# Two of four column transposes moved from TensorE to the DMA engines, with the head-row moves split over two queues

## Chip, cores, metric

One core of a Trainium2 chip. The metric is the device time of one execution in microseconds (us). TensorE is called PE, VectorE DVE, ScalarE ACT, GpSimd POOL or Pool, SyncE SP.

## The reference

```python
xn = layernorm(A_x)                                # 2048 rows of 512, bf16
# branch A: 32 heads of 16; each row attends to 8 rows before it, 2 apart
q, k, v = split(xn @ wqkv)
s = softmax(masked(q . k[i - 2w], w = 0..7) * 0.25) @ v[i - 2w]  @ wo
# branch B: layernorm, gelu(. @ w1), row shifts, @ w2, residual,
#           layernorm, gelu(. @ w3) @ w4, residual, silu
out = x + s * silu(B(xn))
```

## The kernel before

The rows are split by parity into two halves (p = 0, 1) of 1024, each in two chunks of 512. Chunks 0 and 1 are half 0, chunks 2 and 3 half 1. Queries and keys, and branch B's `w1`, need the normed rows as columns (`xnT`). PE makes all four chunks' columns by multiplying with the identity:

```python
def stage_t(c, h):                  # half a chunk: 8 PE transposes, one copy out
    ...
    for j in range(2):
        for dt in range(ND):
            nc.tensor.transpose(pt[:, dt, j, :], x_c[:, 2 * h + j, dt * P : (dt + 1) * P], ident[:])
    copy(out=xnT[p][:, :, t0 : t0 + 2 * P], in_=pt.rearrange("p a j q -> p a (j q)"))

def stage_m(c):                     # DVE: columns times the second norm's factor, for w1
    nc.vector.tensor_tensor(out=xn2T[c], in0=xnT[p][:, :, cs], in1=rrep..., op=ALU.mult)
```

The scores work on 32-row groups of which 16 rows are one head's and 16 the mask's. DVE fills whole tiles with the mask (`mask_fill`), and then small DMAs, the head-row moves, put the heads of `kq` into them, 64 to 72 KB each:

```python
def spread(p, lo, hi, q=nc.sync, ws=(0, 1)):       # w: keys, queries; 8 moves for each
    for w in ws:
        for e in range(2):
            for gr in range(4):
                r = 32 * gr + DH * e
                q.dma_start(out=(kT, qT)[w][e][r : r + DH, :, lo:hi], in_=kq[p][w][r : r + DH, :, lo:hi])
```

Issue order of the part in question (each engine runs its own instructions in this order):

```python
    stage_w1(0, 0); stage_t(1, 0); stage_t(1, 1)
    ln_stats(2); ln_again(2); stage_w1(0, 1)
    mask_fill(0); spread(0, 0, CH); ln_norm(2)            # 16 moves on SP
    ...                                                   # projections of chunk 1
    stage_t(2, 0); stage_t(2, 1)
    ln_stats(3, 0, 2); ln_stats(3, 2, 4); ln_norm(3); ln_again(3)
    stage_w1(1, 0); stage_w1(1, 1); stage_r(2); stage_m(2)
    qk_pair(2, 0); stage_t(3, 0); stage_t(3, 1); qk_pair(2, 1)
    stage_w1(2, 0, lambda: stage_r(3)); stage_m(3)
    mask_fill(1); spread(0, CH, X)                        # 16 moves on SP
    stage_w1(2, 1); load_w3(); stage_w1(3, 0); stage_w1(3, 1)
    va = values(0, 0)
    # then the first attention pass: 8 units of scores, values, w2 tiles, projections
```

The later feed-forward stage already makes columns by DMA: rows to a DRAM scratch (`x1n_dram`), and a transposing DMA back.

The softmax here doesn't subtract the row's maximum and nothing guards it: scores larger than these inputs give would overflow.

## Time and profile before

| | before |
|---|---|
| median time, all runs | 206.55 us |
| profiled span | 204.8 us, clock 0.998 |
| PE transposes of chunks 2 and 3 | 0.89 and 0.90 us |
| first score group of the first pass | 44.57 to 44.93 us |
| first pass from there to the feed-forward | 44.93 to 88.41 us |

The span runs from the first to the last instruction; the device time is 1.8 us longer. The prediction below shows the lines.

### The profile page before, as it was taken

Reading aid. Unit: us, or ns where it says so; the run is one execution under the profiler, and the core shown is the slowest. Engines: PE = TensorE matmul, PEld = TensorE weight load, DVE = VectorE, ACT = ScalarE, POOL = GpSimd, SP = SyncE. Lnnn points to the kernel's source line nnn. Section 1 sums busy time; section 2 is a strip of 40 time slices with the busy share of each in tenths; the row PEclk is TensorE's granted clock in tenths of the full one; section 3 lists DMA queues with packets and bytes.
Section 4 is the critical chain, followed back from the end, with each engine's and each line's share of the span. In section 5 each row is a group of like instructions: output and inputs, shape, how many; then the busy total and the mean of one; then the engine's idle time right before and its main releaser. Section 6 shows DMA issues by size and latency. Waiting matters only on the chain.

```text
span 204.8 us, 4854 instructions
## 1 busy us (share of the span) xinstructions
PE 197.3 (96%) x1944; PEld 95.6 (47%) x1944; DVE 135.2 (66%) x256; ACT 132.7 (65%) x160; POOL 74.1 (36%) x145
## 2 busy tenths in 40 slices
PE   7799999999999999999999999999999999999990
PEld 2475455444444444544444444444455544444440
DVE  5788996545487986776940001188577968888693
ACT  2366788868968687885556557898788877212130
POOL 4798465000032294933791000003830590700000
PEclk9999999999999999999999999999999999999999
DMA  5992065067900399485779948695130241554312
GB/s 131 361 349 84 15 101 96 0 97 113 293 10 0 108 121 151 86 212 105 180 178 215 286 145 134 93 254 193 34 54 3 52 92 26 122 162 135 95 51 77
DMA packets 30590, 25.69 MB, mean 125 GB/s; under 512 B 12505, under 2 KB 28481, under 8 KB 30569
## 3 DMA queue, kind: packets, MB, share of 16 engines
q1 hardware_dynamic: 28376, 22.17, 43.0%
q0 software_dynamic: 2048, 3.09, 8.9%
q8 instruction: 15, 0.25, 0.5%
q10 hardware_dynamic: 144, 0.13, 0.2%
q14 instruction: 7, 0.05, 0.1%
HBM read 12.40 MB, written 4.46 MB: 82 GB/s over the span
## 4 chain that ended last, share of the span: by engine, by line
PE 87%; ACT 4%; DVE 4%; POOL 1%; DMA 1%; issue 1%
PE w_ps L511 19%; PE w_ps L491 19%; PE qk_ps L391 8%; PE v_ps L537 7%; PE w_ps L424 7%; PE s_ps L557 6%; PE w_ps L447 6%; PE wo_ps L673 6%; PE o_ps L580 4%; PE qk_ps L409 4%; ACT arena L562 3%; PE tr_ps L353 1%; DMA arena<-in_A_x_dram 1%; ACT arena L414 1%; DVE l0s L304 1%; POOL l0r L308 1%
## 5 line engine op out<-in xcount | busy, mean ns | idle before, releaser
L562 ACT ACTIVATE arena<-s_ps 128x960 bf16<-128x960 f32 (+1 forms) x68 | 62.9, 979 | 14.4 <-PE s_ps L557 14.4
L511 PE MATMUL w_ps<-arena 128*128 128x512 bf16 (+1 forms) x164 | 39.1, 380 | 0.0
L496 ACT ACTIVATE arena<-w_ps 128x1024 bf16<-128x1024 f32 x20 | 20.5, 1023 | 15.0 <-PE w_ps L491 14.3
L491 PEld LDWEIGHTS <-arena 128*128 128x128 bf16 (+1 forms) x176 | 17.5, 100 | 20.6 <-issue 0.4
L622 POOL DMA_DIRECT2D arena<-orw x48 | 24.9, 527 | 5.8 <-DVE orw L592 5.8
L511 PEld LDWEIGHTS <-arena 128*128 128x128 bf16 (+1 forms) x176 | 16.5, 98 | 19.6
L683 POOL TENSOR_TENSOR arena<-arena 128x512 bf16<-128x512 bf16 x6 | 7.7, 1301 | 44.5 <-DVE arena L681 44.5
L526 ACT ACTIVATE sig<-arena 128x512 bf16<-128x512 bf16 x16 | 10.1, 630 | 20.8 <-DVE arena L517 20.7
L541 DVE CAST v_aug<-v_ps 128x512 bf16<-128x512 f32 x17 | 11.7, 688 | 14.6 <-PE v_ps L537 14.6
L592 DVE CAST orw<-o_ps 128x960 bf16<-128x960 f32 (+1 forms) x17 | 19.7, 1156 | 2.5 <-PE o_ps L580 2.4
L491 PE MATMUL w_ps<-arena 128*128 128x512 bf16 (+1 forms) x88 | 19.5, 379 | 0.1
L491 PE MATMUL w_ps<-arena,arena 128*128 128x512 bf16 (+1 forms) x88 | 19.2, 379 | 0.0
L391 PE MATMUL qk_ps<-arena 128*128 128x512 bf16 (+1 forms) x104 | 18.6, 330 | 0.5 <-ACT arena L321 0.5
L537 PE MATMUL v_ps<-wv_sb,arena 128*128 128x512 bf16 x68 | 17.5, 380 | 0.1
L557 PEld LDWEIGHTS <-arena 32*128 32x128 bf16 x544 | 10.1, 92 | 14.5 <-issue 14.4
L273 POOL TENSOR_SCALAR l3r<-l3m 128x1 f32<-128x1 f32 (+1 forms) x10 | 2.2, 222 | 39.0 <-DVE l3m L282 39.0
L557 PE MATMUL s_ps<-arena 32*128 32x120 bf16 (+1 forms) x544 | 15.8, 214 | 0.0
L447 PE MATMUL w_ps<-arena 128*128 128x512 bf16 x64 | 15.7, 380 | 0.1
L517 DVE TENSOR_TENSOR arena<-w_ps,arena 128x512 bf16<-128x512 f32 x16 | 11.0, 686 | 7.2 <-PE w_ps L511 7.2
L650 DVE TENSOR_TENSOR arena<-arena,orw 128x1440 bf16<-128x1440 bf16 (+1 forms) x2 | 1.6, 784 | 20.5 <-DMA orw<-rden_d 20.5
L424 PE MATMUL w_ps<-arena 128*128 128x512 bf16 x64 | 14.6, 379 | 0.0
L451 DVE TENSOR_TENSOR arena<-w_ps,arena 128x512 bf16<-128x512 f32 x16 | 10.7, 686 | 4.1 <-PE w_ps L447 4.1
(98 smaller groups left out, 278.9 us busy)
## 6 DMA issues: line engine op xcount, KB each, us to landing
x1n_dram<-arena SPq DMA_DIRECT2D x4, 512.0 KB, 3.0
arena<-in_A_x_dram SPq DMA_DIRECT2D x4, 512.0 KB, 6.1
arena<-in_A_x_dram SPq DMA_DIRECT2D x6, 256.0 KB, 7.0
out_dram<-arena SPq DMA_DIRECT2D x6, 256.0 KB, 3.0
arena<-in_B_w_dram SPq DMA_DIRECT2D x1, 1376.0 KB
arena<-in_B_w_dram SPq DMA_DIRECT2D x1, 1280.0 KB
arena<-arena SPq DMA_DIRECT2D x16, 72.0 KB, 2.6
arena<-arena SPq DMA_DIRECT2D x16, 68.0 KB, 3.5
```

Of the source, the lines that this page charges most:

```text
L391: nc.tensor.matmul(pt[:, b, hh * w : (hh + 1) * w], lhsT=wqk_sb[:, dt, nt * P : (nt + 1) * P], rhs=xnT[p][:, dt, k * CH + hh * w : k * CH ...
L424: nc.tensor.matmul(pt[:, b, :], lhsT=w1_sb[:, dt, g * P : (g + 1) * P], rhs=xn2T[c][:, dt, :], start=(dt == 0), stop=(dt == ND - 1),)
L447: nc.tensor.matmul(pt, lhsT=w2_src(p, g, m0), rhs=w2_sb[:, g, :], start=(g == 0), stop=(g == ND - 1))
L491: nc.tensor.matmul(pt[:fs, ft % 2, :], lhsT=w3_sb[:, dt, ft * P : ft * P + fs], rhs=x1nT[c][:, dt, :], start=(dt == 0), stop=(dt == ND - 1),)
L496: nc.scalar.activation(h3(c, 2 * a, 2), pt, AF.Gelu_apprx_tanh)
L511: nc.tensor.matmul(pt, lhsT=h3(c, ft, 1)[:fs, 0, jj * P : (jj + 1) * P], rhs=w4_sb[:fs, ft, :], start=(ft == 0), stop=(ft == NF - 1),)
L537: nc.tensor.matmul(vp[:nk, :], lhsT=xnT[p][:, dt, k0 : k0 + nk], rhs=wv_sb[:, dt, :], start=(dt == 0), stop=(dt == ND - 1),)
L557: nc.tensor.matmul(st[:nk, b, i * nq : (i + 1) * nq], lhsT=kT[e][r : r + 32, dt, k0 : k0 + nk], rhs=qT[e][r : r + 32, dt, q0 : q0 + nq], s ...
L562: nc.scalar.activation(prv[:nk, 2 * h : 2 * h + 2], st[:nk, :, 0 : 4 * nq], AF.Exp, scale=SCALE)
L592: nc.vector.tensor_copy(out=orw[p, r][:, :, :, q0 - ra : q0 - ra + nq], in_=op[:, :, 0 : 4 * nq].rearrange("p j (s q) -> p j s q", q=nq),)
L622: nc.gpsimd.dma_start(out=oT[p][DH * hh : DH * (hh + 1), :, ra : ra + rw], in_=orw[p, r][32 * cg : 32 * cg + DH, jj],)
L673: nc.tensor.matmul(pt, lhsT=oT[p][:, dt, i * P : (i + 1) * P], rhs=wo_sb[:, dt, :], start=(dt == 0), stop=(dt == ND - 1),)
```

## The change

Its intent: take 32 transposes off PE; norm chunks 2 and 3 earlier, so that their longer way through DRAM is hidden; give Pool most of the head-row moves, because SP now issues the transposes; move three projections out of the attention pass and regroup it; load the exp table ahead of the first exp.

```diff
+    def turn_dma(c, lo=0, hi=TPC):
+        rows = x1n_dram[c * CH + lo * P : c * CH + hi * P, :]
+        nc.sync.dma_start(out=rows..., in_=xn[p][:, k * TPC + lo : k * TPC + hi, :])
+        return lambda: nc.sync.dma_start_transpose(
+            out=xnT[p][:, :, k * CH + lo * P : k * CH + hi * P], in_=rows)
 ...
     stage_t(1, 0)
     stage_t(1, 1)
-    ln_stats(2)
+    ln_stats(2, 2, 4)
+    mask_full(0)
+    ln_norm(2)
+    turn_dma(2)()
     ln_again(2)
 ...
+    ln_norm(3, slice(0, 1))
+    turns = [turn_dma(3, 0, 2)]
+    ln_stats(3, 2, 4)
+    mask_fill(0, (0,))
+    ln_norm(3, slice(1, 2))
+    turns.append(turn_dma(3, 2, 4))
+    for f in turns:
+        f()
+    ln_again(3)
+    spread(0, 0, CH, nc.gpsimd, (0,))
 ...
-    stage_t(2, 0)
-    stage_t(2, 1)
 ...
+    mask_fill(0, (1,))
+    spread(0, 0, CH, nc.gpsimd, (1,), (0,))
     qk_pair(2, 0)[0]()
-    stage_t(3, 0)
-    stage_t(3, 1)
     qk_pair(2, 1)[0]()
+    spread(0, 0, CH, nc.sync, (1,), (1,))
+    mask_fill(1, (0,))
+    spread(0, CH, X, nc.gpsimd, (0,))
 ...
+    spread(0, CH, X, nc.sync, (1,))
     stage_w1(2, 1)
+    qk_pair(2, 2)[0]()
 ...
+    qk_one(2, 6)
+    nc.scalar.preload_act_table_set("exp_and_others")
-        (("www", "qq"), ("q", "ww"), ("qw", "qw"), ...)
+        [("www", "qw")] + [("q", "ww")] * 6 + [("q", "q")]
```

(Cut: moved statistics and mask pieces, `values(0, 0)` moved ahead of `stage_r(2)`, shifted places of a few small items in the pass and of one pair of later moves, the start of one buffer rotation.)

More of the change, by code (lines that the diff above doesn't have):

```diff
@@ L113 @@
     sg_at = (61, 66, B0 + 33.5)
-    cnt = {"v": 0, "p": 1, "b": 0, "r": 0, "g": 0}
+    cnt = {"v": 0, "p": 0, "b": 0, "r": 0, "g": 0}
     def pst(tag, name):
@@ L238, in mask_full, with mask_fill @@
         )
-    def mask_fill(k):
-        for w in range(2):
+    def mask_fill(k, ws=(0, 1)):
+        for w in ws:
             for e in range(2):
@@ L247, in mask_fill, with spread @@
                     )
-    def spread(p, lo, hi, q=nc.sync, ws=(0, 1)):
+    def spread(p, lo, hi, q=nc.sync, ws=(0, 1), es=(0, 1)):
         for w in ws:
-            for e in range(2):
+            for e in es:
                 for gr in range(4):
@@ L321, in first_t, with ln_norm @@
         nc.scalar.copy(out=xnT[0][:, :, j * P : (j + 1) * P], in_=pt)
-    def ln_norm(c):
+    def ln_norm(c, part=slice(None)):
         p, k = c // 2, c % 2
         x_c = xn[p][:, k * TPC : (k + 1) * TPC, :]
-        for lo, hi, mv, rstd in lns[c]:
+        for lo, hi, mv, rstd in lns[c][part]:
             for j in range(lo, hi):
@@ L356, in stage_t @@
         copy(out=xnT[p][:, :, t0 : t0 + 2 * P], in_=pt.rearrange("p a j q -> p a (j q)"))
+    def turn_dma(c, lo=0, hi=TPC):
+        p, k = c // 2, c % 2
+        rows = x1n_dram[c * CH + lo * P : c * CH + hi * P, :]
+        nc.sync.dma_start(
+            out=rows.rearrange("(i q) d -> q i d", q=P), in_=xn[p][:, k * TPC + lo : k * TPC + hi, :]
+        )
+        return lambda: nc.sync.dma_start_transpose(
+            out=xnT[p][:, :, k * CH + lo * P : k * CH + hi * P], in_=rows
+        )
     def stage_x():
@@ L726 @@
     ln_norm(1)
-    mask_full(0)
-    mask_full(1)
     parts[1][1]()
@@ L731 @@
     qk_pair(0, 3)[0]()
+    ln_stats(2, 0, 2)
     stage_w1(0, 0)
@@ L734 @@
     stage_t(1, 1)
-    ln_stats(2)
+    ln_stats(2, 2, 4)
+    mask_full(0)
+    ln_norm(2)
+    turn_dma(2)()
     ln_again(2)
     stage_w1(0, 1)
-    mask_fill(0)
-    spread(0, 0, CH)
-    ln_norm(2)
+    ln_stats(3, 0, 2)
+    mask_full(1)
     for a in range(2):
@@ L747 @@
     stage_x()
-    stage_t(2, 0)
-    stage_t(2, 1)
-    ln_stats(3, 0, 2)
-    ln_stats(3, 2, 4)
-    ln_norm(3)
-    ln_again(3)
     stage_w1(1, 0)
     stage_w1(1, 1)
+    va = values(0, 0)
     stage_r(2)
     stage_m(2)
+    mask_fill(0, (1,))
+    spread(0, 0, CH, nc.gpsimd, (1,), (0,))
     qk_pair(2, 0)[0]()
-    stage_t(3, 0)
-    stage_t(3, 1)
     qk_pair(2, 1)[0]()
+    spread(0, 0, CH, nc.sync, (1,), (1,))
+    mask_fill(1, (0,))
+    spread(0, CH, X, nc.gpsimd, (0,))
     stage_w1(2, 0, lambda: stage_r(3))
     stage_m(3)
-    mask_fill(1)
-    spread(0, CH, X)
+    mask_fill(1, (1,))
+    spread(0, CH, X, nc.sync, (1,))
     stage_w1(2, 1)
+    qk_pair(2, 2)[0]()
     load_w3()
@@ L769 @@
     stage_w1(3, 1)
-    va = values(0, 0)
+    qk_one(2, 6)
+    nc.scalar.preload_act_table_set("exp_and_others")
     groups = {n: ([], []) for n in range(len(order))}
@@ L778 @@
     w2q = [lambda t=t: w2_and(t) for t in range(S // P)]
-    qkq = [lambda t=t: qk_one(2 + t // 8, t % 8) for t in range(4, 16)]
+    qkq = [lambda t=t: qk_one(2 + t // 8, t % 8) for t in range(7, 16)]
     for n, (a, b) in enumerate(
-        (("www", "qq"), ("q", "ww"), ("qw", "qw"), ("q", "ww"), ("qw", "qw"), ("q", "ww"), ("qw", "qw"), ("q", "w"))
+        [("www", "qw")] + [("q", "ww")] * 6 + [("q", "q")]
     ):
@@ L796 @@
     st3(3, 4)
-    st3(4, 5, 6, 7)
+    st3(4, 5, 6)
+    st3(5, 7)
     late[6] += [lambda: ln3_norm(1), lambda: normalise_dn(0, 1), lambda: ln3_turn(1)]
@@ L834 @@
     for w in range(2):
-        late[3 + w].append(lambda w=w: spread(1, 0, CUT, nc.gpsimd, (w,)))
+        late[3 + 2 * w].append(lambda w=w: spread(1, 0, CUT, nc.gpsimd, (w,)))
     prev = None
```

## The prediction

> **What bounds the kernel now.** I read four views, in this order: the page's busy shares and slices, the table of windows, the timeline by engine from 20 to 66 us, and the DMA records. The page first:
>
> ```profile
> PE 197.3 (96%) x1944; PEld 95.6 (47%) x1944; DVE 135.2 (66%) x256; ACT 132.7 (65%) x160; POOL 74.1 (36%) x145
> ...
> PE   7799999999999999999999999999999999999990
> ...
> DMA  5992065067900399485779948695130241554312
> ...
> PE 87%; ACT 4%; DVE 4%; POOL 1%; DMA 1%; issue 1%
> ```
>
> The reader is to see that TensorE (PE) is busy from slice 3 to the end and carries 87% of the chain that ended last; no other engine passes 66%. A microsecond taken from PE is therefore a microsecond of the kernel, unless something new makes PE wait. The changed stretch in the table of windows (us; then busy PE, PEld, DVE, ACT, POOL):
>
> ```profile
> 27.57:28.46 0.89, 0.89 (x17) 0.89 (x16) 0.89 (x2) 0.69 (x1) 0.71 (x1) 1.00 0.64 101
> 33.86:34.76 0.90, 0.90 (x18) 0.90 (x17) 0.90 (x2) 0.70 (x1) 0.69 (x1) 1.00 0.61 106
> 34.76:44.57 9.81, 9.81 (x51) 4.44 (x49) 4.46 (x10) 7.37 (x9) 1.16 (x1) 1.00 0.26 41
> 44.57:88.41 43.84, 43.58 (x625) 20.95 (x625) 32.52 (x56) 35.70 (x46) 18.26 (x39) 1.00 0.57 115
> ```
>
> The first two rows are exactly the PE transposes of chunk 2 and of chunk 3. The granted clock is 1.00 throughout. From 12.4 to 44.57 us PE runs back to back, and the first attention pass then fills 44.57 to 88.41.
>
> **What the Trainium skill says.** (1) "VectorE: DVE Perf Modes", section "The three transpose paths": a 128x128 bf16 transpose is 390 ns on TensorE, 1309 ns by DMA. For PE the trace is far lower in a row: 16 start in 0.89 us, 56 ns each. For the DMA way the trace has the later stage of the same kernel, which bounces normed rows through DRAM and transposes 512x512 back:
>
> ```profile
> L473 SPq DMA_DIRECT2D x1n_dram<-arena x4: 389/394/398, 69.2 to 105.6; - x4
> ...
> L478 SPq DMA_TRANSPOSE arena<-x1n_dram x4: 1863/2465/2894, 72.2 to 109.1; - x4
> ```
>
> And from the view of the transposing line alone:
>
> ```profile
> DMA to landing us min/median/max: 4.3/4.6/5.0
> ```
>
> The store needs 3.0 us (page, median) and the transpose 4.3 to 5.0, so columns arrive about 7.5 us after the norm. Latency, not throughput, is what this costs.
>
> (2) "SBUF — State Buffer", section "SBUF: two separate sides": while VectorE runs a 2-port copy, GpSimd is locked out and cannot write descriptors for DMAs it issues. The trace agrees for GpSimd's arithmetic, against the normal 0.23 us of the first operation:
>
> ```profile
> 22.89 1.13 POOL L273 TENSOR_SCALAR l1r<-l1m 128x4 f32<-128x4 f32 x1 [2.52 <-DVE l1m L282]
> 24.10 1.37 POOL L274 TENSOR_TENSOR l1r<-l1r,nhalf 128x4 f32<-128x4 f32 x1
> ```
>
> They lie beside four VectorE mask copies (22.72 to 25.19). For Pool-issued DMAs beside such copies the trace has no case: its Pool moves took 0.52 us each in a part without them.
>
> (3) "DMA: Bandwidth & Descriptors", section "Issuing engines are not separate DMA queues": a second issuing engine saves only sequencer time. The SP queue spends 0.59 us on each head-row move:
>
> ```profile
> 23.46 27.28 SPq L254 DMA_DIRECT2D arena<-arena  x32
> ```
>
> 32 x 0.59 = 19 us of SP time. That is why the transposes cannot simply go behind those moves on SP, and the change gives 20 of the 32 to Pool.
>
> (4) "ScalarE: Activation LUTs", section "What ACT_TABLE_LOAD costs": about 1283 ns for the load. The trace agrees, and shows that the wait before it is small:
>
> ```profile
> 43.87 1.03 ACT L428 ACTIVATE arena<-w_ps 128x1024 bf16<-128x1024 f32 x1 [0.70 <-PE w_ps L424]
> 45.05 1.28 ACT L562 ACT_TABLE_LOAD   x1 [0.15 <-PE s_ps L557]
> 46.35 1.94 ACT L562 ACTIVATE arena<-s_ps 128x1024 bf16<-128x1024 f32 x2
> ```
>
> **The change part by part.**
>
> Removed from PE: 32 transposes, 0.89 + 0.90 = 1.79 us, all on the path. From ACT go four copies of 128x1024 (two pairs of about 1.95 us) off the path, from SP 20 issues.
>
> Moved: three of the twelve query/key projections of the attention pass, and the first values tile. These keep their PE time (4 x 0.216 = 0.86 us each); they only change place. I walked PE's new order with those durations. Until 23.9 us nothing moves. Then: projections of chunk 1 to 27.57; the two w1 pairs to 31.02 (before: 31.91); values 31.9; the rrep matmuls of chunk 2 at 31.9 to 32.15; **chunk 2's columns first needed at 32.15**; two pairs to 35.6; w1 of chunk 2 to 39.3; the pair moved ahead to 41.0; **chunk 3's scaled columns needed at 41.0**; w1 of chunk 3 to 44.45; one projection to 45.3; **first scores at about 45.35**, needing the head rows.
>
> Chunk 2's supply: its statistics end near 21.1 (four tiles at 0.80 us, split around the copy that waited for PE until 18.9), a mask piece of 0.6 us follows, and Pool's second rstd allows the last norms at about 23.2. Store issued 23.3, landed 26.3 (the DMAs are quiet there: 0 in the fifth slice, and the moves of the sixth are gone), transpose landed 30.6 to 31.3. Margin 0.9 to 1.5 us before 32.15.
>
> Chunk 3's supply: first half normed about 27.6, second half about 31.1 (VectorE's order: statistics, rrep product, norms, two mask copies of 0.62). SP issues the second store at 31.2, it lands near 34, the last transpose lands near 38 to 39, the VectorE product (1.22 us) ends 39.3 to 40.2. Margin 0.8 to 1.7 us.
>
> Head rows: Pool reaches its 8 key moves near 33, after the last r2b; at 0.53 us they would end at 37.3. Then come a copy (0.86) and 4 query moves, to 40.3 undisturbed; landing took 2.4 us on SP and a median 5.0 on Pool, so 42.7 to 45.3 against 45.35. VectorE runs about ten mask copies between 34 and 41 us. If each blocks Pool for part of its 0.25 to 0.62 us, two or three us are added, and the first scores wait 0 to 2 us.
>
> exp table: it now stands behind gelu and one more projection copy (0.59 us). I put the first exp 2.0 us after the first scores; before it was 1.78 (46.35 - 44.57). No gain; what offsets it is that ScalarE has one copy less inside each of the units that had two.
>
> Attention pass: PE's pure work in 44.57 to 88.41 is 16 w2 tiles, 12 projections and 8 values at 0.86 us (31.1), 16 score groups at 0.35 (5.6) and 7 weighted groups at 0.53 (3.7): 40.4 of 43.84. The other 3.4 us are 0.37 to 0.57 per unit. Units with one projection and two w2 tiles had 0.37 (61.97 to 67.02), those with two of each 0.43 (67.02 to 73.00), and the new grouping makes nearly all units of the first form. I count 0.3 us gained.
>
> Sum: 206.55 - 1.79 - 0.3 = 204.46 with every supply in time. For waits I add 0.55: as estimates, head rows about 0.35 (a one in two chance of some 0.7), columns about 0.2. **204.46 + 0.55 = 205.0.** The wide feed-forward, the second pass and the tail, 88.41 to the end, run the same instructions in the same order, so nothing is won or lost there.
>
> **The rivals.**
> A, clean: everything lands in time, 204.2 to 204.6. For it: both margins come out positive with measured durations. Against: each is about 1 us behind a chain of seven or more steps, and the DMAs are shared with the Pool moves from 33 us on.
> B, the first scores take over the wait: the Pool moves are delayed by the mask copies and the first score group waits for a DMA. Two us of wait would give about 206.5, all of the gain gone. For it: the blocked Pool operations above and the 5.0 us landing. Against: nothing in the old trace shows a blocked Pool DMA, and the early norms and the split over queues look like a schedule fitted to a trace.
> C, the columns come late: the chunk 2 transpose lands after 32.15, or chunk 3's after about 39.8. A transpose slower by 2 us (the old store to transpose gap varied from 3.0 to 5.8 us with its neighbours) costs about 1 us: 205.5.
> D, VectorE becomes the bound of a unit: 5.05 us per unit holds 0.69 + 1.15 + two sums of 0.69 + up to two statistics at 0.84, near 4.9. Where norms (1.4) fall in as well, PE may wait a few tenths per unit: 205.0 to 205.5. For it: VectorE was busy 4.96 of the 5 us from 65 to 70. Against: PE did not wait there.
>
> **Range and chances.** A weighs 0.4, the others share the rest, and they can add up. That spreads from 204.1 (a cleaner pass than I count) to 206.6 (B at its full size). The removed PE work bounds the gain: over 2% would need 202.4, 2.3 us below the clean sum with 0.3 us of smoothing, and I see nothing of that size. Over 2% slower, 210.7, would need 6 us of new waits. Chances: faster 0.02, same 0.95, slower 0.03.
>
> **What would show it.** Right: no transposes by PE after 20 us, the PE total down by about 1.8 us, the first scores near 45.4, the first pass about 41 us long, and the stretch from the feed-forward on unchanged in length. Transposes landing before PE asks show the columns in time; a PE gap before the chunk 2 projections or w1 of chunk 3 shows C; one before the first scores, with Pool DMA instructions above 0.53 us, shows B; PE gaps inside units with VectorE full show D. The first exp no earlier than 1.8 us after the first scores shows that the table load brought nothing. I am wrong if the pass after 88 us changes length, or if PE gains more than the transposes it lost.

## The result

| | before | after |
|---|---|---|
| median of 4 runs | 206.56 us | 208.25 us (208.05 to 209.02) |
| ratio | 1 | 1.0088, interval 1.0063 to 1.0114 |
| profiled span | 204.8 us | 205.9 us |

The ratio is the mean time of one kernel's runs over that of the other's of the same rounds, so not quite the ratio of the medians. Executions over 1.5% slower than the fastest of the same kernel are left out of the means. PE lost its transposes, and the kernel became slower. The changed kernel's page:

```profile
PE 195.9 (95%) x1912; PEld 94.0 (46%) x1912; DVE 135.0 (66%) x256; ACT 129.7 (63%) x155; POOL 85.1 (41%) x169
...
PE   7799999968999999999999999999999999999990
...
PE 77%; DMA 7%; POOL 7%; DVE 6%; issue 1%; ACT 0%; POOLq 0%
```

There are 32 matmuls fewer and 1.4 us less of PE's busy time, and in the ninth and tenth slices (41 to 51 us) two digits, 6 and 8, where there were nines. PE's timeline of the changed kernel there (start, duration, instruction; in brackets the idle time ahead and what ended it):

```profile
39.27 1.89 PE L401 MATMUL qk_ps<-arena 128*128 128x512 bf16 x8
42.92 3.63 PE L434 MATMUL w_ps<-arena 128*128 128x512 bf16 x16 [1.76 <-DVE arena L385]
46.38 1.03 PE L419 MATMUL qk_ps<-arena 128*128 128x512 bf16 x4
47.34 0.40 PE L567 MATMUL s_ps<-arena 32*128 32x128 bf16 x8
48.03 0.22 PE L567 MATMUL s_ps<-arena 32*128 32x128 bf16 x1 [0.30 <-DMA arena<-arena]
48.71 0.38 PE L567 MATMUL s_ps<-arena 32*128 32x128 bf16 x7 [0.45 <-DMA arena<-arena]
```

And the first scores in the kernel before, which did not wait:

```profile
44.57 0.42 PE L557 MATMUL s_ps<-arena 32*128 32x128 bf16 x16
44.93 2.84 PE L447 MATMUL w_ps<-arena 128*128 128x512 bf16 x12
```

Two new waits: 1.9 us before w1 of chunk 3 (from 41.0, where PE's own pace would have started it, to 42.92; the view says 1.76, as it lets the last matmul end later), which needed DVE's scaled columns (L385) and so the transposed ones; and 1.3 us within the first scores (47.34 to 49.02, against 0.36 before), which needed head-row moves. No stretch after that has a new wait. First the old kernel's table of windows, then the new one's:

```profile
44.93:88.41 43.48, 43.22 (x614) 20.69 (x609) 32.27 (x56) 35.37 (x45) 18.26 (x39) 1.00 0.57 115
88.41:127.20 38.79, 38.79 (x211) 17.93 (x213) 13.74 (x31) 23.80 (x25) 11.53 (x22) 1.00 0.75 181
```

```profile
49.02:89.56 40.54, 40.41 (x599) 19.57 (x597) 32.03 (x56) 32.87 (x41) 18.29 (x40) 1.00 0.62 118
89.56:128.35 38.79, 38.79 (x212) 17.93 (x214) 13.80 (x31) 24.28 (x26) 11.62 (x22) 1.00 0.77 186
```

The pass is 2.94 us shorter, of which 3 x 0.86 = 2.59 is the work moved ahead: 0.35 us gained by the grouping. The feed-forward is 38.79 us in both. So the whole loss lies before 49.02 us. By my walk the first scores should have ended at 45.35 + 0.36 = 45.7; they ended 3.3 us later. 3.3 - 1.79 - 0.35 = 1.16, and the span grew by 1.1 us. (Some 0.3 us more lies outside the span: time minus span is 2.15 us here and 1.8 before. It came and went among the experiments, between 1.8 and 2.2, and I did not find what it hangs on.)

What was late? The changed kernel's chain of waits runs, in this stretch, through Pool and its moves:

```profile
33.68 1.01 POOL r2b L343
...
36.60 5.50 DMA arena<-arena
42.11 0.28 issue
42.39 6.28 DMA arena<-arena
48.66 0.04 issue
48.71 0.38 PE s_ps L567 x7
```

The twelfth Pool move, issued at 42.39 us because it had to wait until the fourth had landed, took 6.28 us. The 64 KB moves of the kernel before, issued by SP alone with no transpose beside them, landed in a median 2.4 us. The gap before w1 of chunk 3 is not on this chain: it lies inside the wait for the moves.

The columns were late in two ways. Pool's timeline of the changed kernel:

```profile
25.84 1.78 POOL L274 TENSOR_TENSOR l1r<-l1r,nhalf 128x2 f32<-128x2 f32 x1
30.10 1.13 POOL L273 TENSOR_SCALAR l1r<-l1m 128x2 f32<-128x2 f32 x1 [2.47 <-DVE l1m L282]
31.31 0.71 POOL L274 TENSOR_TENSOR l1r<-l1r,nhalf 128x2 f32<-128x2 f32 x1
33.68 1.01 POOL L343 TENSOR_TENSOR r2b<-r,nhalf 128x4 bf16<-128x4 f32 x1 [1.65 <-DVE r L340]
34.64 4.78 POOL L254 DMA_DIRECT2D arena<-arena  x8
```

Two rstd operations take 1.78 and 1.13 instead of 0.73 and 0.22 us; they lie beside DVE's product (25.83 to 27.05) and its mask copies (29.93 to 31.2). Chunk 3's last norm ended at 32.8 us instead of the 31.1 that I had counted. And the second half's transpose, issued by SP at 35.34, was landed when DVE went on at 41.64:

```profile
35.34 1.28 SPq L364 DMA_TRANSPOSE arena<-x1n_dram x1
41.64 1.23 DVE L385 TENSOR_TENSOR arena<-arena 128x2048 bf16<-128x2048 bf16 x1 [3.66 <-DMA arena<-x1n_dram]
```

That is 6.3 us for half a chunk, where chunk 3's first half had taken 4.1 and chunk 2's whole one 4.6 (26.52 to 31.12).

### The profile page after: what moved, and what is told of

Its sections match the earlier page's. It is cut to its first block, busy times and chain, and to the rows that moved or that the text cites. A ratio compares the mean times of both kernels' runs of the same rounds, so it can differ in the third digit from the quotient of the medians.

```text
span 205.9 us, 4800 instructions
## 1 busy us (share of the span) xinstructions
PE 195.9 (95%) x1912; PEld 94.0 (46%) x1912; DVE 135.0 (66%) x256; ACT 129.7 (63%) x155; POOL 85.1 (41%) x169
## 4 chain that ended last, share of the span: by engine, by line
PE 77%; DMA 7%; POOL 7%; DVE 6%; issue 1%; ACT 0%; POOLq 0%
PE w_ps L521 19%; PE w_ps L501 19%; PE v_ps L547 7%; PE w_ps L457 7%; PE s_ps L567 7%; PE wo_ps L683 6%; DMA arena<-arena 6%; PE o_ps L590 4%; PE qk_ps L419 4%; PE qk_ps L401 3%; POOL l1r L274 2%; DVE l1s L281 1%; DMA arena<-in_A_x_dram 1%; POOL l1r L273 1%; POOL r2b L343 1%
## 5 line engine op out<-in xcount | busy, mean ns | idle before, releaser
L254 POOL DMA_DIRECT2D arena<-arena x36 | 19.1, 535 | 5.0 <-DMA arena<-arena 2.1
L401 PE MATMUL qk_ps<-arena 128*128 128x512 bf16 (+1 forms) x112 | 20.4, 333 | 0.5 <-ACT arena L321 0.5
L567 PE MATMUL s_ps<-arena 32*128 32x120 bf16 (+1 forms) x544 | 16.5, 213 | 0.7 <-DMA arena<-arena 0.7
L408 ACT CAST arena<-qk_ps 128x1024 bf16<-128x1024 f32 x11 | 11.1, 1017 | 6.1 <-PE qk_ps L401 6.1
```

What stands on the lines that cost most here:

```text
L401: nc.tensor.matmul(pt[:, b, hh * w : (hh + 1) * w], lhsT=wqk_sb[:, dt, nt * P : (nt + 1) * P], rhs=xnT[p][:, dt, k * CH + hh * w : k * CH ...
L567: nc.tensor.matmul(st[:nk, b, i * nq : (i + 1) * nq], lhsT=kT[e][r : r + 32, dt, k0 : k0 + nk], rhs=qT[e][r : r + 32, dt, q0 : q0 + nq], s ...
```

## The experiments

**Theory M** (moves): the Pool moves set the end of the wait, and moves and transposes slow each other down on the DMA engines they share. **Rival S**: the two waits add up, each with its own cause. **Rival C**: the columns are late by themselves, through the late norms. A later refinement, **theory R**: what stretches a transpose is moves from Pool's queue in flight beside it; moves on SP's own queue hardly do. All runs of the kernel before beside these gave medians of 206.47 to 206.54 us.

### e1_mask_late: the mask copies out of Pool's way

```diff
     ln_stats(3, 2, 4)
-    mask_fill(0, (0,))
     ln_norm(3, slice(1, 2))
     ...
     ln_again(3)
+    mask_fill(0, (0,))
```

> Theory M (the last Pool query move sets the end of the wait, and the 1.9 us gap before w1 of chunk 3 lies inside it): the two mask copies now come behind the last norms of chunk 3, so Pool's rstd operation falls from 1.13 to about 0.23 us and these norms end near 31.8 instead of 32.8 us; the gap before w1 of chunk 3 shrinks from 1.9 to about 0.9 us, but the first scores then wait about 1 us longer for the same landing near 48.7 us, and the time stays within 0.3 us of 208.2. Theory S (the two waits add up): the time falls by about 1 us, to 207.2.

Measured: 207.92 us median, four runs from 206.53 to 210.58 (one slow); fast-run ratio 1.0043, interval 0.9993 to 1.0092. Pool's operation fell to 0.22 us and the second store went out at 31.7 us. PE's timeline of this run:

```profile
40.83 3.62 PE L434 MATMUL w_ps<-arena 128*128 128x512 bf16 x16
44.28 1.03 PE L419 MATMUL qk_ps<-arena 128*128 128x512 bf16 x4
45.48 0.23 PE L567 MATMUL s_ps<-arena 32*128 32x128 bf16 x1 [0.18 <-DMA arena<-arena]
...
47.81 0.38 PE L567 MATMUL s_ps<-arena 32*128 32x128 bf16 x7 [0.48 <-DMA arena<-arena]
48.12 4.24 PE L457 MATMUL w_ps<-arena 128*128 128x512 bf16 x12
```

The first wait is gone entirely, and the second grew from 1.3 to 2.5 us (45.3 to 48.12, less 0.36). The scores ended 0.9 us earlier in this trace (48.12 instead of 49.02), as Pool began its moves 0.8 us earlier (33.86 instead of 34.64). So the 1.9 us that were removed did not count in full, against S; and that nothing would be gained, as M had it, was wrong too. The times alone decide nothing: the traced run is the slowest of the three fast ones (208.73), and the two others, 206.53 and 207.11, lie 1.1 to 1.7 us below the changed kernel's median and have no trace. And another cost came in: the twelve matmuls at 48.12 took 4.24 us instead of 2.84. The table of windows gives the granted clock (third figure from the end):

```profile
48.12:52.15 4.03, 4.03 (x15) 1.52 (x13) 1.38 (x2) 1.17 (x2) 0.44 (x1) 0.64 1.05 111
```

After the waits PE was granted 0.64 of its clock for 4 us. A wait on PE can so cost more than its length, and not in every run: that would fit the wide spread, but only one of the four runs was traced.

### e3_no_moves: no early moves at all (wrong)

```diff
-    spread(0, 0, CH, ...)      # all three calls
-    spread(0, CH, X, ...)      # both calls
-    ... AF.Exp, scale=SCALE
+    ... AF.Exp, scale=1e-7
```

> Wrong result on purpose: the 32 early head-row moves are left out, and the exp gets a tiny scale so that nothing overflows. Theory M: both waits come from the moves, the first by contention on the DMA engines (the second half transpose landed 6.3 us after its issue, the whole one of chunk 2 took 4.1), the second because the scores need them. Without them the last transpose lands in about 4 us, the gap before w1 of chunk 3 is at most 0.3 us, the first scores start near 45.4 us, and the time is 204.6 to 205.0. Rival C (the columns are late by themselves, through the late norms): a gap of about 1 us or more stays before w1 of chunk 3 and the time is 205.7 to 206.2.

Measured: 204.52 us (204.46 to 204.82), ratio 0.9904. The norms ended as late as in the changed kernel (32.8), but DVE had the columns at 39.86 instead of 41.64, w1 of chunk 3 started at 41.14, 0.1 us behind PE's own pace, and the first scores ran from 45.57 without a wait. The late norms alone (rival C) cost PE 0.1 us. My prediction's clean sum, 204.46, is about what the kernel does without the moves.

### e2_pe_chunk3 and e4_pe_both: one, or both, transposed by PE again

```diff
-    turns = [turn_dma(3, 0, 2)]; turns.append(turn_dma(3, 2, 4)); for f in turns: f()
     qk_pair(2, 0)[0]()
+    stage_t(3, 0)
+    stage_t(3, 1)
     qk_pair(2, 1)[0]()
```

and in e4_pe_both also `turn_dma(2)` out, `stage_t(2, 0)` and `stage_t(2, 1)` behind `stage_x`.

> Chunk 3 is transposed by TensorE again (0.9 us more of it), chunk 2 still by DMA; the rest as in the changed kernel. Theory M with contention as its cause: the moves have the DMA engines to themselves, land by about 45 us, no gap stays and the first scores start near 46.3 us: 205.6 to 206.0. If Pool's late start (34.6 us) and its issue times alone delay the moves, the first scores still wait until 47 us or later: 206.5 to 207.5.

Measured: 205.33 us (205.22 to 205.42), ratio 0.9941, interval 0.9925 to 0.9958. No wait is left: the first scores start at 46.09 us. Pool started its moves at 34.43 us, no earlier than in the changed kernel, but they landed in a median 3.9 us instead of 6.1. The DMA views from 33 to 50 us, of the changed kernel and then of this one:

```profile
arena<-arena POOLq DMA_DIRECT2D x12, 64.0 KB, 6.1
arena<-arena POOLq DMA_DIRECT2D x12, 64.0 KB, 3.9
```

So it is not Pool's start or issue time alone that made them late, but the company of chunk 3's transposes. The 3.9 us are still more than the 2.4 of the kernel before, where one queue issued all moves: moves from two queues are company for each other too.

> Both chunks by TensorE as before, everything else of the change kept (early norms, moves shared by Pool and SP, regrouped first pass, table load ahead). PE has 1.8 us more than in the changed kernel, the first scores come near 47.2 us with their rows in place: 206.55 minus the 0.35 us that the regrouping won in the trace, so 206.1 to 206.4. If the moves are late by themselves: 207 or more.

Measured: 205.86 us (205.82 to 206.12), ratio 0.9968. The first scores start at 47.04 us, without a wait. This is the change without its transposes: it gains 0.7 us, of which the pass shows 0.35 (47.39 to 87.93 is 40.54 us, as in the changed kernel). Chunk 2 by DMA is worth 0.5 us beside that (205.86 to 205.33), not PE's whole 0.9: the pass of e2 took 40.84 us instead of 40.54 (46.45 to 87.29), and why is open.

### e5_sp_only: the sharing of the moves undone

```diff
-    spread(0, 0, CH, nc.gpsimd, (0,))
+    spread(0, 0, CH, nc.sync, (0,))        # and likewise the other two Pool calls
```

> The changed kernel with the sharing undone: all 32 early moves are issued by SP, behind the transposes. If the sharing by itself made the moves late (Pool's start at 34.6 us, its waits, the software queue), the first scores start earlier than 48.7 us and the time falls below 207.8. If what counts is that moves and transposes share the DMA engines and that SP starts moves only after the last transpose (36.7 us, 16 moves at 0.59 us and some 3 us to land), the first scores start near 49 to 50 us: 208.5 to 209.8, and sharing was worth keeping.

Measured: 210.2 us (209.89 to 210.53), ratio 1.0171. The first scores ended at 49.40 us, 0.4 us later than with sharing, as the second theory had it; a second wait of 2.2 us, which I had not foreseen, came at 102.46 us, where the feed-forward's second chunk waited for its transposed columns; its cause was not looked for. So sharing was right, given where the moves stood. The run shows something else too: no Pool move is in flight, the second half's transpose was issued at 35.08 and DVE went on at 39.17:

```profile
39.17 1.23 DVE L385 TENSOR_TENSOR arena<-arena 128x2048 bf16<-128x2048 bf16 x1 [1.27 <-DMA arena<-x1n_dram]
```

That is 4.1 us instead of 6.3, although SP issued moves from 36.4 us on, behind it. That gave theory R. (Fewer moves were in flight as well: four by 39.17, against eleven from Pool and four from SP by 41.64 in the changed kernel.)

### e7_whole_chunk3: chunk 3 in one piece

```diff
-    turns = [turn_dma(3, 0, 2)] ... turns.append(turn_dma(3, 2, 4)) ...
+    turn_dma(3)()                          # behind the last norm
```

> The changed kernel with chunk 3 stored and transposed as one piece, behind its last norms. Columns come 0.5 to 1 us later (store at 32.8 us, about 3 us, then 4.1 us plus some 2 us of contention), so the gap before w1 of chunk 3 grows to 2.3 to 3 us; theory M says that the first scores start at 48.7 us as before or a little earlier or later with the traffic, and the time stays within 0.5 us of 208.2. If instead the gap itself is paid, it rises by as much, to 208.8 or more. Beside that: the time minus the profiled span is 2.1 us in the three kernels with half transposes and 1.8 in the others; if the halves are the reason, it is 1.8 here.

Measured: 211.71 us (210.74 to 212.47), ratio 1.0246: a miss. The transpose took 8.51 us beside the Pool moves (35.98 to 44.49), so now the columns were the later of the two and PE waited 4.7 us for them; behind that w1 of chunk 3 took 5.31 instead of 3.63 us, at a granted clock of 0.67. Theory M as I had put it, "the moves set the end", holds only while the columns come first. The halves of the original were worth 3.5 us, part of it through that clock. (That the halves cause the 0.3 us outside the span is not confirmed: it was 1.9 to 2.1 us here, without them.)

### e6_no_preload: the exp table not loaded ahead

From e2_pe_chunk3:

```diff
-    nc.scalar.preload_act_table_set("exp_and_others")
```

> The kernel with chunk 3 on TensorE (205.33 us), without the early load of the exp table, so that the load stands before the first exp. My prediction's claim: it brought nothing, as the load comes behind the last projection copy and its wait was 0.15 us; the time stays within 0.15 us of 205.33. The change's intent: 0.5 to 1.3 us slower without it.

Measured: 205.35 us (205.28 to 205.65), ratio 0.9944, against 205.33 and 0.9941 with the early load. It brings nothing.

### e9_rearranged and e11_sp_early: the same places, with and without Pool

e9 puts the key masks right behind chunk 2's norms, four key moves on SP behind chunk 2's transpose, chunk 3 in one piece, and all later moves at the end on SP; four key and four query moves stay on Pool. e11 differs from it only so:

```diff
-    turn_dma(3)()                                    # store and transpose
+    turn3 = turn_dma(3)                              # store
+    spread(0, 0, CH, nc.sync, (0,), (1,))            # key moves while it is in flight
+    turn3()                                          # transpose
-    spread(0, 0, CH, nc.gpsimd, (0,), (1,))
 ...
-    spread(0, 0, CH, nc.gpsimd, (1,), (0,))
+    spread(0, 0, CH, nc.sync, (1,), (0,))
```

> Both chunks by DMA, but the first mask copies come right after chunk 2's norms, four key moves go out on SP behind chunk 2's transpose, chunk 3 is one piece, and the moves for the later columns go behind all the others on SP. Theory M: with 12 moves instead of 16 (and none of the 16 later ones) in flight around chunk 3's transpose, the first scores wait for nothing: start near 45.4 us, 204.4 to 204.9, as without moves (204.52). If collisions stay, 205 to 207.

Measured: 212.11 us (211.01 to 212.31), ratio 1.0257: a miss, like e7. Its chain of waits, from chunk 3's store to the landing of its transpose:

```profile
32.19 3.02 DMA x1n_dram<-arena
35.21 0.02 issue
35.22 9.08 DMA arena<-x1n_dram
```

> As e9 (whole chunk 3 by DMA, 9.1 us from issue to landing there), but the eight moves that Pool issued go to SP: the second four key moves while chunk 3's store is in flight, the query moves behind the transpose on the same queue. So no Pool-issued move is in flight beside a transpose. Theory R (it is moves from the other queue, Pool's, interleaved with the transpose's many small packets, that stretch it; moves behind it on SP's own queue do not): it lands about 4.1 to 4.7 us after its issue, near 40 us; no gap or at most 0.5 us before w1 of chunk 3, the query moves land near 44 to 45.5 us, and the time is 204.5 to 205.3, below both kernels. If any move in flight stretches it, from whatever queue, it takes 6 us or more and the time stays above 206.5.

The chain of e11, from the same transpose to DVE's product:

```profile
35.38 5.03 DMA arena<-x1n_dram
40.41 0.03 issue
40.46 0.04 issue
40.50 1.24 DVE arena L385
```

Measured for e11: 205.3 us (205.12 to 205.6), ratio 0.9948. The same transpose, issued at the same time, takes 9.08 us with eight Pool moves in flight and 5.03 us with the moves on SP (four issued before it, of which at least three had not landed, and three behind it before it landed). A gap of 0.8 us is left before w1 of chunk 3, a little more than I expected, and the scores do not wait.

### e12_halves: chunk 3 in halves, key moves in SP's idle times

From e11, chunk 3 in halves again, and key moves in SP's idle times: two while chunk 2's store is in flight, four behind its transpose, one behind each of chunk 3's stores.

```diff
+    turn2 = turn_dma(2)
     mask_fill(0, (0,))
+    spread(0, 0, CH, nc.sync, (0,), (0,), (0, 1))
+    turn2()
 ...
+    spread(0, 0, CH, nc.sync, (0,), (0,), (2, 3)); spread(0, 0, CH, nc.sync, (0,), (1,), (0, 1))
     ln_stats(3, 0, 2); ln_stats(3, 2, 4)
     ln_norm(3, slice(0, 1)); turns = [turn_dma(3, 0, 2)]
+    spread(0, 0, CH, nc.sync, (0,), (1,), (2,))
     ln_norm(3, slice(1, 2)); turns.append(turn_dma(3, 2, 4))
+    spread(0, 0, CH, nc.sync, (0,), (1,), (3,))
     for f in turns: f()
```

> As e11, with chunk 3 in halves and the key moves spread over SP's idle time (two while chunk 2's store is in flight, four behind its transpose, one each behind chunk 3's stores). Theory R: with the second half's store issued near 32.1 us and its transpose near 34.7, landing 4.1 us later as in e5, the columns are there at 38.9 us and the 0.8 us gap of e11 goes; query moves land near 44 us, before the first scores. 204.4 to 204.9, some 0.6 us below e11. If the early moves delay chunk 2's transpose by more than its 0.8 us of slack, or the query moves come later than 45.4 us, 205.3 or more.

Measured: 204.46 us (204.29 to 204.74), correct, ratio to the kernel before 0.9906, interval 0.989 to 0.9923. PE's timeline of it:

```profile
39.05 1.89 PE L401 MATMUL qk_ps<-arena 128*128 128x512 bf16 x8
40.80 3.63 PE L434 MATMUL w_ps<-arena 128*128 128x512 bf16 x16
44.26 1.03 PE L419 MATMUL qk_ps<-arena 128*128 128x512 bf16 x4
45.22 0.42 PE L567 MATMUL s_ps<-arena 32*128 32x128 bf16 x16
```

No gap, and the first scores at 45.22 us: the walk of the prediction, with its waits at zero. That the time equals the clean sum to the digit is chance: 2.1 us lie outside the span here instead of 1.8, and PE came to this stretch 0.2 us earlier than in the changed kernel (23.70 against 23.93 us).

## Why the prediction was wrong

- **PE's removed work, right.** Matmuls fell by 32; the order and pace up to 41.0 us are those of the walk to within 0.1 us.
- **Chunk 2's supply, right.** Store at 23.52, transpose issued 26.52, landed 4.6 us later at 31.1; PE asked at 32.15 and did not wait. (The expectations of e3 and e7 give 4.1 us for it. That was a misreading: 4.1 is the first half of chunk 3.)
- **The pass, the table, the rest, right.** 0.35 us gained instead of 0.3. The first exp came 2.1 us after the first scores began; e6 shows the table load to be worth nothing. The feed-forward is unchanged.
- **Chunk 3's supply, wrong twice.** "Second half about 31.1" was 32.8: I had shown Pool's arithmetic slowed beside mask copies, and did not apply it to Pool's rstd operations in this stretch. "The last transpose lands near 38 to 39" was 41.6: 6.3 us where I counted 4 to 5. e3 and e5 show that the second is the one that mattered: without Pool moves beside it, the same late norms cost 0.1 us.
- **Head rows, the step that failed.** "42.7 to 45.3" for the last landing, plus two or three for blocked descriptors, with a wait of 0 to 2 us weighted down to 0.35; it was 48.7, and 3.3 us behind the planned start. One move took about what I said to issue (eight in 4.78 us, 0.60 each), but the twelfth was through at 42.9 instead of 40.3: Pool began at 34.64 instead of 33, behind the late norms, and each later Pool move waits until the one eight before it has landed (1.1 us for the eleventh and twelfth), so that the delay runs down the queue. And the landing was mis-sized: 6 us from the issue instead of 2.4 to 5.0. The company is the larger part: e2 began its moves as late (34.43), had no transposes of chunk 3 beside them, and no score waited.
- **The error behind both.** I took the durations of transposes and of moves from stretches without the other beside them, and gave rivals B and C separate chances. They were one event: moves and transposes in flight together, each stretching the other. The prediction's sentence "the DMAs are shared with the Pool moves from 33 us on" named it, and the sum did not contain it.

Settled: the moves beside the transposes cost the 3.3 us (e3 takes them away, e2 and e12 separate them); in e1 a start of Pool's moves 0.8 us earlier brought the end 0.9 us forward. Shown by e9 against e11: with the moves on SP instead of Pool the transpose takes 5.03 instead of 9.08 us; the place of the key moves, ahead of the transpose instead of beside it, differs there too, and e5 is the case with moves only behind it. That it is the queue, and not how many moves are in flight, is theory R and not fully separated. For it speaks that chunk 2's transpose took 4.7 us in e9 and e11 with four SP moves behind it, against 4.3 to 4.6 in the runs with none (4.6 in the changed kernel). The packet records of the traces (no view prints them one by one) add this: 64 KB stand there as 16 packets of 4096 bytes when Pool issued them, as 64 of 1024 bytes when SP did. In e9 the transpose's last data packet starts at 40.8 us, Pool's packets take 0.8 to 1.0 of the engines' time from 40.5 to 42.5, and the transpose counts as landed at 44.3; in e11 the two times are 39.9 and 40.4. Open: by what rule the two queues' packets share an engine in these runs, and the 0.3 us outside the span.

## What to carry to other kernels

Before work is moved from a full engine to the DMAs, list what else is in flight in that very stretch, and take durations from a stretch with the same company, not from a quiet one. Put a latency-bound transfer on a queue on which the bulk moves stand behind it, or in its sender's idle times, and compare what arrives last: a gap that lies inside a longer wait is not the one to mend. A wait on PE may also cost clock afterwards (0.64 for 4 us in e1).

## What the Trainium skill lacked or had wrong

- "DMA: Bandwidth & Descriptors", section "Issuing engines are not separate DMA queues", says that the DMAs of all issuers run on the same 16 engines and interleave, and that a second issuing engine saves only sequencer time. The first agrees with these traces; the second is too little, for the choice changed the transfer: a 512x512 transpose took 4.3 to 4.6 us with no move beside it (chunk 2 in e7 and in the changed kernel), 5.03 us with moves on its own SP queue (e11) and 8.51 to 9.08 us with Pool-issued moves in flight (e7, e9). The page has bandwidths for the transpose; I found no figure in it for one beside other transfers.
- "VectorE: DVE Perf Modes", section "The three transpose paths": it gives 390 ns for a block on TensorE; in a row they cost 56 ns each here. 16 such blocks by DMA took 4.6 us, not 16 x 1309 ns, plus 3.0 us for the store to DRAM that the table does not count.
- "SBUF — State Buffer", section "SBUF: two separate sides": its lock agrees with Pool's small arithmetic (1.13 us beside mask copies, 0.22 without, e1). Its 620 to 3100 ns for a Pool-issued DMA beside a copy are for a whole transfer. Here the issue took 0.57 to 0.78 us beside mask copies and 0.51 without, and in e2 the first four moves, issued beside them, landed in 2.4 to 3.3 us; no run has such a move alone, so this tests the figure only in part.
- "TensorE: Matmul & The Clock Gate", section "Part 1: The HAM clock gate (the "warmup" mystery)", ties the loss of clock to an idle window of about 3.4 us. e7 fits: PE stood for 4.7 us, then 0.67. But in e1 PE was still busy for 1.14 of 2.82 us before it, and was then granted 0.64 for 4 us; in the changed kernel's trace a gap of 1.9 us cost no clock. A later section of the page speaks of frequent short idles, without saying how short.
